# Summing spectral products with accumulating DMAs in a convolution and FFN kernel

## The chip, the cores and the metric

The kernel runs on one core of a Trainium2 chip. The metric is the device time in microseconds (us), as the median of several executions. Every set of runs also executed the kernel before on the same chip; its medians there lay between 374.68 and 375.06 us. A run is fast or slow; only fast runs are compared here. The span of a profile is about 1.9 us shorter than the device time of the same execution.

## The reference, cut to what matters

Two layers, each with a long convolution (A) and a gated feed-forward network (B); 2048 rows of 512 columns, 1792 hidden columns.

```python
k_shift = sum over t of k_pad[:, t:t + S, :] * shift_k[:, ks - 1 - t]     # 4 taps
kv = k_shift * v
y = irfft(rfft(kv, padded) * rfft(ssm_k, padded))[:, :S] + kv * ssm_D
A(q) = q * y
B(x) = (silu(x @ w_gate) * (x @ w_up)) @ w_down
x = q
x = x + A(layernorm(x)); x = x + B(layernorm(x))      # layer 0
x = x + A(layernorm(x)); x = x + B(layernorm(x))      # layer 1
```

y depends on k, v and ssm_k only, so the spectral work is done once and both layers use its result.

## The kernel before

The rows are cut into four chunks of 512. Chunk by chunk the kernel transforms kv (spectrum X) and h (ssm_k; spectra H, combined to G) by matmuls with a small Fourier matrix, multiplies spectra, adds the products that belong to the same output chunk into Z, and transforms Z back. This is interleaved with 16 FFN units (two layers, four chunks, two halves of 256 rows). The program is written as a list of operations; a list scheduler, run while the kernel is built, settles the order on every engine from estimated durations and landing times of DMAs. Buffers come from rings of fixed size.

The spectral product, on VectorE, in short form; `sl` covers the four slots, so each operation is 128x2048:

```python
for part in (0, 1):                       # real, imaginary
    t1 = X.real * G[part]                 # dve tensor_mul
    t2 = X.imag * G[1 - part]             # dve tensor_mul
    comb = ALU.subtract if part == 0 else ALU.add
    if first:                             # the first product of this Z
        Z[part] = t1 comb t2              # dve tensor_tensor
    else:
        t1 = t1 comb t2                   # dve tensor_tensor
        Z[part] = Z[part] + t1            # dve tensor_add
```

The FFN side of VectorE, and the DMA transposes that feed it:

```python
# prologue of a unit: normalised rows z, turned by DMA for the gate and up matmuls
add("SP", 1.25, lambda: nc.sync.dma_start_transpose(out=zT..., in_=z...), lat=1.4, slack=SLK)
...
# unit: 8 matmuls (128x256) per gate or up tile, silu and copy on ScalarE, then
dve(n * W, lambda: nc.vector.tensor_mul(out=ht.t[:], in0=ht.t[:], in1=sg.t[:]), [sg], [ht])
# down projection reads ht
```

h is turned with TensorE and the shift of k is four diagonal matmuls per tile, in all chunks.

Of the kernel before, what the change touches and what calls it, by code (L numbers as in the profile page):

```python
# [19 lines left out]
SLK = 5.0  # L20
PD_ACT, KV_ACT, ST_ACT = True, True, False
HSL = 3.0
Z_ACT, N_ACT = False, False
# [3 lines left out]

BLOCKS = [("C", 0, 1), ("C", 1, 1), ("C", 2, 1), ("C", 3, 1),
# [6 lines left out]
class Buf:  # L35


    def __init__(self, ring, name, make, parts=1):
        self.ring, self.name, self.make, self.parts = ring, name, make, parts
        self.last_write = [None] * parts  # L40
        self.readers = [[] for _ in range(parts)]
        self.ops, self.left, self.free_at, self.t = [], 0, 0.0, None


class Op:
    __slots__ = ("eng", "cost", "lat", "emit", "bufs", "preds", "succs", "due", "fixed", "conv", "left", "end", "start", "n")


class Plan:
# [6 lines left out]
    def __init__(self, rings):  # L56
        self.ops = []
        self.rings = rings
        self.slots = {r: [None] * n for r, n in rings.items()}
        self.queue = {r: [] for r in rings}  # L60
# [6 lines left out]
    def add(self, eng, cost, emit, r=(), w=(), lat=None, due=None, conv=False, slack=0.0):  # L67
        o = Op()
        o.eng, o.cost, o.emit, o.conv, o.n = eng, cost, emit, conv, len(self.ops)
        o.lat, o.fixed, o.due = lat, due, -slack  # L70
        o.preds, o.succs, o.bufs = {}, [], []
# [16 lines left out]
        for b in o.bufs:  # L88
            b.ops.append(o)
            b.left += 1  # L90
        for q in o.preds:
            q.succs.append(o)
        o.left = len(o.preds)
# [8 lines left out]
    def dues(self, stretch, floor):  # L102
        nxt = {}
        for o in reversed(self.ops):
# [4 lines left out]
            if o.conv:  # L109
                d = min(d, nxt.get(o.eng, 1e9) - o.cost * stretch[o.eng])  # L110
                nxt[o.eng] = d
                d = max(d, floor)
            o.due = d - slack

    def order(self, warm_until, warm):
        t = {e: 0.0 for e in self.SAME}
        ready = {e: [] for e in self.SAME}
        for o in self.ops:
            if not o.left:
                ready[o.eng].append(o)  # L120
        done = 0
        heads = {r: 0 for r in self.rings}
        while done < len(self.ops):
            best = None
            for e, cand in ready.items():
                pick = None
                for o in cand:
# [3 lines left out]
                    ok = True  # L131
                    taken = {}
                    for b in o.bufs:
                        if b.t is None and b.ring != "one":
                            qd = self.queue[b.ring]
                            if heads[b.ring] >= len(qd) or qd[heads[b.ring] + taken.get(b.ring, 0)] is not b:
                                ok = False
                                break
                            free = sorted(s.free_at if s is not None else 0.0 for s in self.slots[b.ring]
                                          if s is None or not s.left)  # L140
                            n = taken.get(b.ring, 0)
                            if n >= len(free):
                                ok = False
                                break
                            taken[b.ring] = n + 1
                            est = max(est, free[n] + 0.1 if free[n] else 0.0)
# [10 lines left out]
            e = o.eng  # L157
            if e == "PE" and est < warm_until and est - t[e] > 0.5:
                self.dummy(warm, t[e], est)
            for b in o.bufs:  # L160
                if b.t is None and b.ring == "one":
                    b.t = b.make(0)
                if b.t is None:
                    slot = min((i for i, s in enumerate(self.slots[b.ring]) if s is None or not s.left),
                               key=lambda i: self.slots[b.ring][i].free_at if self.slots[b.ring][i] is not None else 0.0)
                    self.slots[b.ring][slot] = b
                    heads[b.ring] += 1
                    b.t = b.make(slot)
            o.emit()
            o.start, o.end = est, est + o.cost  # L170
            t[e] = o.end
            for b in o.bufs:
                b.left -= 1
                b.free_at = max(b.free_at, o.end + (0.15 if o.lat is None else o.lat))
            ready[e].remove(o)
            for s in o.succs:
                s.left -= 1
                if not s.left:
                    ready[s.eng].append(s)
            done += 1  # L180

    def dummy(self, warm, a, b):
        for ring in ("pf", "pd", "pc"):
            for i, s in enumerate(self.slots[ring]):
                if s is None or (not s.left and s.free_at <= a):
                    n = int((b - a - 0.4) / 0.085)
                    if n > 0:
                        warm(ring, i, n)
                    return
# [3 lines left out]
def kernel(  # L193
# [29 lines left out]
    o_t = out.rearrange("b s d -> (b s) d").rearrange("(c p r) d -> p c r d", p=P, r=R)  # L223
    k3 = A_k.rearrange("b s d -> (b s) d").rearrange("s (dt p) -> s dt p", p=P)
# [7 lines left out]
                 "sg": 2, "ht": 5, "st": 8, "mv": 6, "ve": 6, "rs": 6, "pf": 4, "pc": 2, "pd": 2})  # L232
# [26 lines left out]
    NI = NT // 2  # L259
    m4, fq = whole("m4", [P, R], F32), whole("fq", [P, P], F32)  # L260
# [3 lines left out]
    fwd, inv = whole("fwd", [P, NT, P]), whole("inv", [P, NT, P], parts=2)  # L264
# [8 lines left out]
    hn, kT, vt, xs = {}, {}, {}, {}  # L273

    def load_h(b, eng="SP", due=None):
        hn[b] = new("h", "hn", [P, KD, L], parts=1)
        q = nc.sync if eng == "SP" else nc.scalar
        add(eng, 0.55, lambda: q.dma_start(out=hn[b].t[:], in_=h3[:, :, b * L:(b + 1) * L]), w=[hn[b]], lat=4.5, due=due)

    def load_k(b, due=None):  # L280
        kT[b] = new("k", "kTb", [P, KD, PADL + L], parts=2)
        if b == 0:
            add("POOL", 0.2, lambda: nc.gpsimd.memset(kT[b].t[:, :, 0:PADL], 0.0), w=[(kT[b], (0,))])
            add("SP", 1.5, lambda: nc.sync.dma_start_transpose(out=kT[b].t[:, :, PADL:PADL + L], in_=k3[0:L]),
                w=[(kT[b], (1,))], lat=3.5, due=due)
        else:
            add("SP", 2.2, lambda: nc.sync.dma_start_transpose(out=kT[b].t[:], in_=k3[b * L - PADL:(b + 1) * L]),
                w=[kT[b]], lat=4.0)

    def load_v(b, due=None):  # L290
        vt[b] = new("v", "vt", [P, R, D], parts=R)
        add("SP", 0.6, lambda: nc.sync.dma_start(out=vt[b].t[:], in_=v_t[:, b]), w=[vt[b]], lat=4.5, due=due)

    def load_x(c, due=None):
        xs[c] = new("x", "xc", [P, R, D], parts=R)
        add("SP", 0.7, lambda: nc.sync.dma_start(out=xs[c].t[:], in_=q_t[:, c]), w=[xs[c]], lat=4.5, due=due)
# [91 lines left out]
    def shift_mul(b, ring, conv):  # L388
        for r in range(R):
# [7 lines left out]
            add("PE", pe(KS * KD, P), go, r=[kT[b], dg], w=[ps], conv=conv)  # L397
# [19 lines left out]
    def fold2(src, dst, conv):  # L417

        for lo, op in ((0, ALU.add), (2, ALU.subtract)):
            dve(4 * D, lambda lo=lo, op=op: nc.vector.tensor_tensor(out=dst.t[:, lo:lo + 2], in0=src.t[:, 0:2],  # L420
                                                                    in1=src.t[:, 2:4], op=op),
                [src], [(dst, key((lo, lo + 1)))], conv=conv)
# [14 lines left out]
    def forward4(rows, name, scale, ring, conv):  # L437
        ev = spectrum(name)
        by_residue(rows, ev, scale, ring, ("ACT",), conv)
        m = spectrum("m")  # L440
        fold2(ev, m, conv)
# [4 lines left out]
    def spectrum_h(b, ring="pc"):  # L446
        hs = transpose_h(b, ring, (0, 2), True)
        h, hp = forward4(hs, "H", 2.0 / N, ring, True), H[b - 1]
        H[b] = h
# [5 lines left out]

# [399 lines left out]
```

## Time and profile before

| | before |
|---|---|
| device time, median | 374.69 us |
| span of the profile | 372.8 us |
| first 128x512 gating product (end of unit 1) | 59.73 us |
| from there to the eleventh (units 2 to 11) | 213.8 us |
| units 12 to 16 | 92.6 us |
| tail | 6.6 us |

Each unit ends on VectorE with the one narrow gating product, ht 128x512, so the starts of these sixteen operations cut any of these kernels into comparable pieces. All stage lengths below are read in this way. In the lines of the profile PE is TensorE, PEld its weight loads, DVE VectorE, ACT ScalarE, POOL GpSimd and SP SyncE; a q after the name marks instructions that only issue. zT is z turned by DMA, hs and kc are h and k turned; a transfer's landing is its end, counted here from its issue. In the middle piece spectral work and FFN share the engines; in units 12 to 16 only the FFN is left. The lines of the page and of the views are shown in the prediction below. The page's DMA rows: 40 equal slices of the span; the digit is the busy tenths of the 16 DMA engines, below it what they moved.

```profile
DMA  8995050010210441010100230001100210011100
GB/s 243 402 304 155 9 113 25 2 28 2 51 64 1 87 119 51 3 28 3 28 29 1 43 99 2 2 1 31 29 30 0 58 29 2 14 16 15 43 2 28
```

In slices two and three, 90% busy or more with loads, the DMA engines move 402 and 304 GB/s. After the opening the DMA engines are mostly idle.

### The profile page before, as it was taken

The numbers are of one execution on the slowest core, as the hardware profiler recorded it, in microseconds if no ns is written. First come the engines' busy times: TensorE is split into PE (matmuls) and PEld (weight loads), VectorE is DVE, ScalarE is ACT, GpSimd is POOL, SyncE is SP. The second block draws the span as 40 slices with busy tenths as digits, with TensorE's granted clock in tenths as the row PEclk, the third lists the DMA queues.
The fourth block names the chain that finished last, engine by engine and source line by source line (L and its number), as shares of the span: only waits on it lengthen the run. The fifth ranks groups of instructions, "written<-read, shape, count | busy, mean of one in ns | idle before, by whom it ended". The sixth has DMA issues, their size and how long they took to land.

```text
span 372.8 us, 6865 instructions
## 1 busy us (share of the span) xinstructions
PE 354.1 (95%) x2814; PEld 258.9 (69%) x2814; DVE 292.8 (79%) x542; ACT 209.0 (56%) x363; POOL 36.2 (10%) x42
## 2 busy tenths in 40 slices
PE   7989999979999899998999999997999999999995
PEld 7735877747678567766676687775777777777772
DVE  7895999999989999999999799799974453636121
ACT  3668784536684663635456856744456454545452
POOL 1101010110101300111110100021100100100000
PEclk9999999999999999999999999999999999999999
DMA  8995050010210441010100230001100210011100
GB/s 243 402 304 155 9 113 25 2 28 2 51 64 1 87 119 51 3 28 3 28 29 1 43 99 2 2 1 31 29 30 0 58 29 2 14 16 15 43 2 28
DMA packets 34351, 20.42 MB, mean 55 GB/s; under 512 B 26384, under 2 KB 32272, under 8 KB 34320
## 3 DMA queue, kind: packets, MB, share of 16 engines
q1 hardware_dynamic: 32736, 19.45, 19.9%
q10 hardware_dynamic: 1584, 0.53, 0.6%
q8 instruction: 22, 0.36, 0.4%
q14 instruction: 9, 0.07, 0.1%
HBM read 11.80 MB, written 2.10 MB: 37 GB/s over the span
## 4 chain that ended last, share of the span: by engine, by line
DVE 45%; PE 41%; DMA 4%; POOL 3%; ACT 3%; issue 1%; SPq 1%; ACTq 0%; POOLq 0%
PE pf L255 24%; PE pd L685 12%; DVE bnst L550 6%; DVE m L420 5%; DVE ht L678 5%; PE ps L255 4%; POOL rstd L555 3%; DVE t L486 3%; DVE t L489 3%; DMA hn<-in_A_ssm_k_dram 3%; DVE t L498 2%; DVE Z L500 2%; DVE Z L495 2%; DVE n L598 2%; DVE z L598 2%; DVE xc L695 1%
## 5 line engine op out<-in xcount | busy, mean ns | idle before, releaser
L255 PE MATMUL pf<-zT,wg_sb 128*128 128x256 bf16 x896 | 116.1, 273 | 1.4 <-DMA zT<-z 1.4
L255 PE MATMUL pf<-zT,wu_sb 128*128 128x256 bf16 x896 | 116.1, 273 | 0.0
L685 PE MATMUL pd<-wd_sb,ht 128*128 128x512 bf16 x448 | 106.6, 379 | 8.1 <-DVE ht L678 8.1
L671 ACT ACTIVATE sg<-pf 128x512 bf16<-128x512 f32 x112 | 67.2, 600 | 74.0 <-PE pf L255 69.9
L255 PEld LDWEIGHTS <-wg_sb 128*128 128x128 bf16 x896 | 87.3, 98 | 22.4 <-DMA zT<-z 1.9
L255 PEld LDWEIGHTS <-wu_sb 128*128 128x128 bf16 x896 | 87.6, 98 | 11.8
L675 ACT CAST ht<-pf 128x512 bf16<-128x512 f32 x112 | 65.8, 587 | 27.5 <-PE pf L255 27.5
L685 PEld LDWEIGHTS <-ht 128*128 128x128 bf16 x448 | 42.8, 98 | 54.0 <-DVE ht L678 12.6
L678 DVE TENSOR_TENSOR ht<-ht,sg 128x1024 bf16<-128x1024 bf16 x64 | 39.5, 617 | 37.9 <-ACT ht L675 37.9
L555 POOL TENSOR_TENSOR rstd<-ve,nhalf 128x2 f32<-128x2 f32 (+1 forms) x33 | 35.1, 1064 | 304.6 <-DVE ve L553 304.6
L550 DVE BATCH_NORM_STATS2 bnst<-xc 128x6 f32<-128x512 bf16 x64 | 41.6, 684 | 1.1 <-DMA xc<-in_A_q_dram 0.5
L692 ACT CAST dn<-pd 128x512 bf16<-128x512 f32 x32 | 17.6, 591 | 23.0 <-PE pd L685 23.0
L489 DVE TENSOR_TENSOR t<-X,G 128x2048 bf16<-128x2048 bf16 x18 | 21.9, 1217 | 0.0
L486 DVE TENSOR_TENSOR t<-X,G 128x2048 bf16<-128x2048 bf16 x18 | 21.9, 1216 | 0.0
L325 ACT ACTIVATE X<-ps 128x512 bf16<-128x512 f32 x32 | 18.5, 599 | 5.5 <-PE ps L255 5.4
L695 DVE TENSOR_TENSOR xc<-xc,dn 128x1024 bf16<-128x1024 bf16 x16 | 11.0, 687 | 10.6 <-ACT dn L692 10.5
L598 DVE TENSOR_SCALAR z<-xc,mv,rstd 128x512 bf16<-128x512 bf16 x32 | 11.8, 409 | 7.3 <-POOL rstd L555 7.2
L598 DVE TENSOR_SCALAR n<-xc,mv,rstd 128x512 bf16<-128x512 bf16 x32 | 12.2, 409 | 6.6 <-POOL rstd L555 6.6
L255 PE MATMUL ps<-dg,kTb 128*128 128x128 bf16 x256 | 15.8, 219 | 0.6 <-ACT Yk L542 0.6
L255 PEld LDWEIGHTS <-kTb 128*128 128x128 bf16 x256 | 15.3, 114 | 1.2 <-issue 0.7
L255 PEld LDWEIGHTS <-fwd 128*128 128x128 bf16 x96 | 9.3, 98 | 8.8 <-issue 0.4
L255 PE MATMUL ps<-vt,fwd 128*128 128x512 bf16 x56 | 15.2, 379 | 0.1
(65 smaller groups left out, 260.1 us busy)
## 6 DMA issues: line engine op xcount, KB each, us to landing
vt<-in_A_v_dram SPq DMA_DIRECT2D x4, 512.0 KB, 4.2
xc<-in_A_q_dram SPq DMA_DIRECT2D x4, 512.0 KB, 4.4
out_dram<-xc SPq DMA_DIRECT2D x16, 128.0 KB, 1.8
wg_sb<-in_B_w_gate_dram SPq DMA_DIRECT2D x1, 1792.0 KB, 10.9
wu_sb<-in_B_w_up_dram SPq DMA_DIRECT2D x1, 1792.0 KB, 15.0
wd_sb<-in_B_w_down_dram SPq DMA_DIRECT2D x1, 1792.0 KB, 19.7
hn<-in_A_ssm_k_dram SPq DMA_DIRECT2D x3, 512.0 KB, 3.3
hn<-in_A_ssm_k_dram ACTq DMA_DIRECT2D x1, 512.0 KB, 3.5
```

Of the source, the lines that this page charges most:

```text
L255: nc.tensor.matmul(o, lhsT=lhsT, rhs=rhs, start=(n == 0), stop=(n == len(terms) - 1))
L325: add("ACT", act(D), lambda: nc.scalar.activation(out=view(), in_=ps.t[:], func=ACT.Copy, scale=scale), r=[ps], w=[(buf, keys)], conv=conv)
L420: dve(4 * D, lambda lo=lo, op=op: nc.vector.tensor_tensor(out=dst.t[:, lo:lo + 2], in0=src.t[:, 0:2], in1=src.t[:, 2:4], op=op), [src], [( ...
L486: dve(n * D, lambda t1=t1, part=part: nc.vector.tensor_mul(out=t1.t[:], in0=x.t[:, sl, 0, :], in1=g.t[:, sl, part, :]), [(x, key(slots, (0 ...
L489: dve(n * D, lambda t2=t2, part=part: nc.vector.tensor_mul(out=t2.t[:], in0=x.t[:, sl, 1, :], in1=g.t[:, sl, 1 - part, :]), [(x, key(slots ...
L550: add("DVE", 0.6, lambda st=st, i=i: nc.vector.bn_stats(out=st.t[:], in_=xs[c].t[:, i, :]), r=[(xs[c], (i,))], w=[st])
L555: add("POOL", 0.75, lambda: nc.gpsimd.tensor_tensor(out=rstd.t[:], in0=ve.t[:], in1=nhalf.t[:].to_broadcast((P, n)), op=ALU.pow), r=[ve, n ...
L598: add("DVE", 0.325, lambda: nc.vector.tensor_scalar(out=view(), in0=xs[c].t[:, i, :], scalar1=mv.t[:, o, 0:1], scalar2=rstd.t[:, o:o + 1], ...
L671: add("ACT", act(D), lambda ps=ps, o=o, sg=sg: nc.scalar.activation(out=sg.t[:, o:o + 2, :], in_=ps.t[:], func=ACT.Silu), r=[ps], w=[(sg, ...
L675: add("ACT", act(D), lambda ps=ps, o=o, ht=ht: nc.scalar.copy(out=ht.t[:, o:o + 2, :], in_=ps.t[:]), r=[ps], w=[(ht, (o // 2,))], due=t0 + ...
L678: dve(n * W, lambda sg=sg, ht=ht: nc.vector.tensor_mul(out=ht.t[:], in0=ht.t[:], in1=sg.t[:]), [sg], [ht], due=t0 + k * step - HSL)
L685: nc.tensor.matmul(pds[o].t[:], lhsT=ht.t[:, q, o * P:(o + 1) * P], rhs=wt["d"].t[:, ft, :], start=(ft == 0), stop=(ft == NF - 1))
```

## The change

Its intent is to relieve VectorE. (1) The sums into Z leave VectorE and are made by DMAs that accumulate in their destination, 512 KB each, on GpSimd's queue. (2) h of chunks 1 to 3 is copied by ScalarE into another layout and turned by DMA transposes. (3) The taps of chunk 3's k are scaled on ScalarE, summed on VectorE and turned by DMA. (4) The opening loads chunk 0's k naturally and turns it on TensorE, issues the taps first, moves h of chunk 0 to second place on ScalarE's queue, loads h and k of chunk 1 early, and adds D's column on GpSimd. (5) The scheduler is rewritten (deadlines by chunk, order and issue apart). Core of the diff, most of it left out:

```diff
+H_DMA = lambda b: b in (1, 2, 3)
+K_ACT = lambda b: b in (3,)
+Z_DMA = lambda i, j: True
...
+    def accumulate(z, sl, slots, part, t):
+        add("POOL", 1.3, lambda: nc.gpsimd.dma_start(out=z.t[:, sl, part, :], in_=t.t[:], accum_op=ALU.add),
+            r=[t, (z, key(slots, (part,)))], w=[(z, key(slots, (part,)))], lat=5.0, conv=True)
...  # in product(), batched case
+            if part and first and Z_DMA(i, j):
+                dve(n * D, lambda: nc.vector.tensor_mul(out=z.t[:, sl, 1, :], in0=x.t[:, sl, 0, :], in1=g.t[:, sl, 1, :]), ...)
+                if part and Z_DMA(i, j):
+                    accumulate(z, sl, slots, part, t1)
...
+            if part and Z_DMA(i, j):
+                accumulate(z, sl, slots, part, t2)
...
+                if Z_DMA(i, j):
+                    accumulate(z, sl, slots, part, t1)
+                    continue
...  # opening
-    load_h(0, "ACT", -60)
+    add("ACT", 1.5, lambda: nc.scalar.activation(out=warm1.t[:], in_=nhalf.t[:], func=ACT.Silu), ...)
     add("ACT", 0.5, lambda: nc.scalar.dma_start(out=tapT.t[:], ...), w=[tapT],
-        lat=2.4, due=-59)
+        lat=2.4, due=-60)
+    load_h(0, "ACT", -59)
     load_k(0, -60)
     load_v(0, -59)
     add("ACT", 0.5, lambda: nc.scalar.dma_start(out=dcol.t[:], ...), w=[dcol], lat=3.0, due=-58)
     load_x(0, -58)
     load_weights("g", -57)
+    load_h(1, "SP", -56.5)
+    load_k(1, -56.4)
```

## The prediction

> **What bounds the kernel now.** I read the busy shares first, then the chain that ended last, then the kernel in two stretches, because a share over the whole span mixes stages.
>
> ```profile
> PE 354.1 (95%) x2814; PEld 258.9 (69%) x2814; DVE 292.8 (79%) x542; ACT 209.0 (56%) x363; POOL 36.2 (10%) x42
> DVE 45%; PE 41%; DMA 4%; POOL 3%; ACT 3%; issue 1%; SPq 1%; ACTq 0%; POOLq 0%
> ```
>
> TensorE looks full, yet the chain spends more of the span on VectorE. Matmul busy time hides small gaps, so I count TensorE work by spacing. In the timeline near the end, where TensorE never waits, eight gate matmuls start 0.87 us after the eight before (0.109 us each), and eight down-projection matmuls take 1.73 us (0.216 us each); a 128-column matmul takes 0.0555 us (16 in 0.89 us in the chain). 1792 gate/up and 448 down matmuls are then 292 us, and everything in program order 348 us of the 372.8 us span.
>
> ```profile
> core 0: us, PE busy (x) PEld busy (x) DVE busy (x) ACT busy (x) POOL busy (x), PEclk, DMA share, GB/s
> 59.70:273.60 213.90, 204.79 (x1614) 150.06 (x1611) 201.76 (x342) 120.64 (x212) 25.46 (x20) 1.00 0.13 31
> 273.60:366.20 92.60, 92.22 (x705) 68.90 (x705) 39.37 (x91) 48.79 (x84) 5.55 (x8) 1.00 0.11 21
> ```
>
> The cuts are ends of FFN units. There are 16 (two layers, four chunks, two halves), and each ends on VectorE with the one narrow gating product, ht 128x512: the first starts at 59.73 us, the eleventh at 273.56, the last at 366.20. Ten units take 213.9 us with VectorE busy 94%; the last five take 92.6 us with VectorE 43% and TensorE full. So VectorE sets the pace up to 273 us and TensorE after it. How VectorE does that, at the end of the first unit:
>
> ```profile
> 56.65 1.42 DVE L433 TENSOR_TENSOR X<-m 128x512 bf16<-128x512 bf16 x4
> 58.00 0.68 DVE L678 TENSOR_TENSOR ht<-ht,sg 128x1024 bf16<-128x1024 bf16 x1
> 58.60 1.21 DVE L495 TENSOR_TENSOR Z<-t,t 128x2048 bf16<-128x2048 bf16 x1
> 59.73 0.42 DVE L678 TENSOR_TENSOR ht<-ht,sg 128x512 bf16<-128x512 bf16 x1
> ```
>
> Spectral work and the gating products share one in-order queue without a gap; TensorE's down projection needs ht, so each 1.2 us operation in front of it is paid.
>
> **What the Trainium skill says.** "Perfetto Trace Analysis", Identifying the Most-Contended Engine, calls matmul busy share a poor measure; the trace agrees (the gate group's mean of 273 ns against 109 ns spacing). "DMA: Bandwidth & Descriptors", SWDGE vs HWDGE vs iDMA, says that accumulating during a DMA is possible only on GpSimd's software path; no run here shows it yet. The same page, Anatomy of one DMA, fits a transfer as about 2.0 us plus bytes over 436e3 per us: 3.2 us for 512 KB. As an accumulating one must also read its destination, I estimate 4 to 6 us from issue to landing; loads of that size in this trace take 3.3 to 4.4 us. "SBUF — State Buffer", Who interferes with whom, says that GpSimd's SBUF reads contend with a two-input VectorE operation. The trace agrees: the small pow on GpSimd takes 0.70 us alone and 1.54 us in the busy stretch.
>
> **The change part by part.**
>
> ```profile
> L489 DVE TENSOR_TENSOR t<-X,G 128x2048 bf16<-128x2048 bf16 x18 | 21.9, 1217 | 0.0
> L500 DVE TENSOR_TENSOR Z<-Z,t 128x2048 bf16<-128x2048 bf16 x12 | 14.6, 1220 | 0.2
> L498 DVE TENSOR_TENSOR t<-t,t 128x2048 bf16<-128x2048 bf16 x12 | 14.6, 1217 | 0.2
> L495 DVE TENSOR_TENSOR Z<-t,t 128x2048 bf16<-128x2048 bf16 x6 | 7.3, 1220 | 0.1
> L255 PE MATMUL ps<-dg,kTb 128*128 128x128 bf16 x256 | 15.8, 219 | 0.6 <-ACT Yk L542 0.6
> L377 PE MATMUL pt<-ident,hn 128*128 128x128 bf16 x64 | 4.9, 220 | 1.7 <-DMA hn<-in_A_ssm_k_dram 1.2 <-DVE hn L740 0.4
> ```
>
> Accumulation: nine batched products. Each of the three that start a Z drops one combination; each of the six others drops the real part's add to Z and both imaginary-part adds. That is 3 + 6 x 3 = 21 operations of 1.22 us, 25.6 us off VectorE, and 21 accumulating DMAs of 512 KB onto GpSimd.
>
> Last shifted k: 64 of the 256 shift matmuls go (3.6 us of TensorE); ScalarE gets 16 scalings of about 0.6 us and loses 4 evacuations; VectorE gets three 1.22 us sums (3.7 us); SyncE gets four transposes.
>
> h by DMA: 48 of 64 transposes leave TensorE (2.7 us), 16 for the natural k arrive (0.9 us); ScalarE's six 1.02 us copies become twelve of about 0.6 us; SyncE gets twelve transposes. A transpose pair of zT takes 2.51 us to issue, so 1.25 us each, and 2.4 us to land.
>
> Where this falls depends on the order, so I cut the built program of both kernels at the 16 unit ends and summed per engine: TensorE by the spacings above; ScalarE by its groups' means; VectorE by the groups' means less 0.03 us. (A plain sum of the means is 314 us against 293 us busy, since neighbours overlap by about 0.055 us; I take half of that, the rest standing for small waits.) The larger of the engines is each unit's length.
>
> Units 2 to 11, before: VectorE 20.8, 22.4, 24.0, 21.1, 19.0, 19.5, 20.3, 23.2, 17.7, 20.2; TensorE 18.2, 21.5, 23.7, 20.0, 17.4, 19.1, 21.1, 24.0, 18.5, 18.2. The larger ones sum to 210.6 us; measured 213.8.
> After: VectorE 17.3, 17.7, 22.7, 20.0, 13.7, 17.7, 21.6, 20.5, 19.0, 16.0; TensorE 16.5, 20.0, 23.5, 20.0, 18.2, 19.1, 21.7, 18.2, 19.1, 19.1. Sum 198.5 us. ScalarE's largest is 19.5, in a unit of 23.5. Gain 12.1 us: VectorE falls under TensorE nearly everywhere, and what is left is TensorE's own 195.4 us.
> Units 12 to 16: TensorE 92.8 before (92.6 measured), 91.9 after; gain 0.9 us. The 6.6 us tail stays.
>
> Opening:
>
> ```profile
> 1.73 6.73 PE L821 MATMUL wm<-ident 128*128 128x128 bf16 x80 [1.73 <-POOL ident masks.py:199]
> 6.69 2.50 DVE L736 TENSOR_TENSOR dg<-ident,tapT 128x512 bf16<-128x512 bf16 x4 [1.47 <-DMA tapT<-in_A_shift_k_dram]
> 18.62 0.50 SPq L278 DMA_DIRECT2D hn<-in_A_ssm_k_dram  x1
> 19.22 8.65 SPq L287 DMA_TRANSPOSE kTb<-in_A_k_dram  x1
> ```
>
> Before, shift matmuls start at 11.2 us, after 80 warming matmuls and the taps' late landing. Afterwards k loads naturally, taps are issued first, and 65 warming matmuls remain; VectorE's order (taps' diagonals split around the phases) lets the shift start at perhaps 9 to 10.5. Two things eat this. Four hr copies of 0.6 us sit between X's evacuations on ScalarE (about 1 us). And hs of chunk 1 now comes from four transposes queued on SyncE behind another k transpose, while the DMA engines are above 90% busy to about 30 us. In order, ScalarE's zT copies stand behind seven of H's evacuations, and TensorE's z transposes behind H's matmuls. Such a transpose held the queue 8.65 us, to 27.9 us; I estimate hs's last block at 28.5 + 3 x 1.25 + 2.4 = 34.7 us, FFN start near 37.5 (38.5 before). I put the first unit's end at 58.5 instead of 59.7, gain 1.2 us.
>
> Accumulation waits, my charge: Z for chunk 2 has two serial imaginary-part accumulations, and VectorE's order leaves about 8 us from the first one's operand to the inverse's first fold; at 5 us each that is 2 us of stall. Chunk 3 leaves 4 us for the last one, in a unit with VectorE slack. Total 1.5 us.
>
> Sum: 374.7 - 12.1 - 0.9 - 1.2 + 1.5 = 362.0 us.
>
> **Rivals.** (1) Accumulation latency becomes the bound. For: they are serial per part of Z, and GpSimd's in-order queue puts later pow operations, which every normalisation needs, behind an issue that waits for an earlier landing. Against: most have 8 to 12 us before the next use. At 8 us each instead of 5, five or six such waits of 2 to 3 us give back 12 us: 373 us. (2) SyncE's queue: hs and kc transposes, 5 us per group, stand before zT transposes, which TensorE waits for. Against: in the trace before, that wait is one of 1.4 us in all. Three late ones of 2 us give 368 us. (3) The opening gains its full 2.5 us or more and no accumulation stalls: 359 us. (4) TensorE was the bound all along, only its removed 5.4 us counting: 369 us. Against: VectorE's 94% and
>
> ```profile
> PE pd L685 <- DVE ht L678: 8.1, 10, 1.2
> ```
>
> waits that busy time shows in part only.
>
> **Range and chances.** The unit sums reproduce the kernel before to 3 us in 306, so the middle is sound to about 3 us if nothing new waits; the opening may miss by 2, the accumulations by up to 8 on the slow side. Hence 355 to 369. The 2% line is 367.2: rival 2 or a mild form of rival 1 is needed to miss it. Faster 0.84, within 0.15, slower 0.01.
>
> **What would show it.** Right: 21 accumulating DMAs and no VectorE add to Z in the batched products, VectorE near 271 us busy, units 2 to 11 in 197 to 203 us, landing of Z's DMAs 4 to 6 us, VectorE under 90% there. Wrong: folds of Z waiting for DMA, pow operations on GpSimd waiting for DMA, zT waits of several us, ScalarE waiting for hs at 30 to 37 us, or the first ht 128x512 not before 59 us.

## The result, and the profile after

The changed kernel takes 392.0 us (median of four, 390.39 to 393.52), the kernel before 374.72 us in the same rounds. The ratio is 1.045 (95% interval 1.039 to 1.051). Ratios here are the mean time of one kernel's fast runs over the mean of the other's fast runs of the same rounds, so not quite the ratio of the medians. The change makes the kernel 17 us slower where I had predicted 13 us faster.

The same two lines of the page as before: busy time by engine, and the chain of work that ended last by engine.

```profile
PE 355.3 (91%) x2668; PEld 257.6 (66%) x2703; DVE 274.8 (70%) x520; ACT 217.2 (55%) x384; POOL 58.3 (15%) x63
PE 56%; DVE 17%; DMA 16%; ACT 6%; issue 3%; POOL 1%; SPq 0%; ACTq 0%; POOLq 0%; DVEq 0%
```

VectorE was relieved as planned: 18 us less busy, and its part of the chain fell from 45% to 17%. But DMA, 4% of the chain before, now has 16%. The two stretches, cut as before (us, then busy time of PE, PEld, DVE, ACT, POOL, then granted clock, DMA share, GB/s):

```profile
66.65:292.50 225.85, 203.15 (x1480) 146.13 (x1500) 182.29 (x323) 127.54 (x227) 47.92 (x42) 0.96 0.54 85
292.50:384.90 92.40, 91.77 (x695) 68.82 (x704) 41.09 (x90) 48.71 (x84) 4.84 (x7) 1.00 0.09 21
```

The middle is 12 us longer, not shorter, with VectorE only 81% busy, the DMA engines at 0.54 instead of 0.13, and a granted clock of 0.96 instead of 1.00. The late stretch is unchanged. The opening is 7 us longer (66.65 against 59.73 us). Set against the prediction, which gave 58.5, 203.2 (213.8 - 12.1 + 1.5), 91.7 and 6.6 us:

| stage | before | predicted | after | after less predicted |
|---|---|---|---|---|
| to the end of unit 1 | 59.7 | 58.5 | 66.7 | +8.2 |
| units 2 to 11 | 213.8 | 203.2 | 225.9 | +22.7 |
| units 12 to 16 | 92.6 | 91.7 | 92.4 | +0.7 |
| tail | 6.6 | 6.6 | 6.9 | +0.3 |

Two errors, then. In the middle the list of waits (who waited for what: us in total, times, longest) has lines that did not exist before:

```profile
POOL Z L593 <- DMA Z<-t: 16.6, 3, 8.1
PE pf L326 <- DMA zT<-z: 11.9, 4, 6.3
DVE t L626 <- DMA Z<-t: 6.8, 3, 3.9
DVE vt L581 <- DMA kc<-ka: 6.7, 1, 6.7
POOL rstd L702 <- DMA Z<-t: 4.7, 1, 4.7
```

Some engines wait for the accumulations themselves (Z<-t); VectorE, which writes t, waits for a product's buffer that an accumulation still reads. TensorE waits for transposes of z that have nothing to do with Z. The chain, read at the start of unit 3 (start, us, what; TensorE's gate and up matmuls in the second line), and the DMA rows of just that unit, 84.3 to 111.2 us, in 40 slices of 0.67 us:

```profile
84.14 7.88 DMA zT<-z
92.16 9.26 PE pf L326 x64
...
DMA  8999999999940002999930000000000100000009
GB/s 137 152 195 187 181 125 125 176 195 196 195 70 0 0 0 40 172 178 171 177 43 0 0 0 0 0 0 0 0 0 0 24 0 0 0 0 12 0 0 188
```

A transpose that takes 2.5 us in the median is issued at 84.14 and lands 7.88 us later. For nearly all of these 7.9 us the DMA engines are full, yet they move only 125 to 196 GB/s, about half of what they moved with loads. Then 64 matmuls take 9.26 us; at the 0.109 us spacing of the prediction they would take 7.0 us. Here "TensorE: Matmul & The Clock Gate" of the Trainium skill, Part 1, The HAM clock gate, tells what I had not looked up: after an idle window of about 3.4 us TensorE's clock is halved until it has been busy for about as long. The trace agrees here: after TensorE's wait of 6.3 us the granted clock is 0.50 from 89.7 to 96.5 us (0.87 over the unit). The gap cost TensorE its own length and some 2 us more. Other gaps in these runs fit the page less well; they come with e17.

Medians of DMA landing (KB, us from issue to landing) from the page; the last two lines concern the opening:

```profile
Z<-t POOLq DMA_DIRECT2D x21, 512.0 KB, 6.4
zT<-z SPq DMA_TRANSPOSE x30, 2.5
kc<-ka SPq DMA_TRANSPOSE x4, 6.8
hn<-in_A_ssm_k_dram ACTq DMA_DIRECT2D x1, 512.0 KB, 10.3
dcol<-in_A_ssm_D_dram ACTq DMA_DIRECT2D x1, 1.0 KB, 12.7
```

The accumulations land after 5.4 to 9.0 us. In the opening h of chunk 0 took 10.3 us to land where it took 3.5 before, and D's column, 1 KB, 12.7 us instead of 5.3. In the timeline of the opening GpSimd's addition of it waits, and behind it the transposes of h and the shift matmuls, which start at 17.80 us instead of 11.20:

```profile
14.62 0.21 POOL L907 TENSOR_TENSOR hn<-hn,dcol 128x4 bf16<-128x4 bf16 x1 [12.85 <-DMA dcol<-in_A_ssm_D_dram]
14.89 1.47 PE L466 MATMUL pt<-ident,hn 128*128 128x128 bf16 x12 [2.67 <-POOL hn L907]
```

### The profile page after: what moved, and what is told of

Read it like the earlier page. It is cut to its first block, busy times and chain, and to the rows that moved or that the text cites. A ratio compares the mean times of both kernels' runs of the same rounds, so it can differ in the third digit from the quotient of the medians.

```text
span 391.8 us, 6690 instructions
## 1 busy us (share of the span) xinstructions
PE 355.3 (91%) x2668; PEld 257.6 (66%) x2703; DVE 274.8 (70%) x520; ACT 217.2 (55%) x384; POOL 58.3 (15%) x63
## 3 DMA queue, kind: packets, MB, share of 16 engines
q1 hardware_dynamic: 39504, 21.55, 22.2%
q0 software_dynamic: 11088, 11.01, 20.4%
## 4 chain that ended last, share of the span: by engine, by line
PE 56%; DVE 17%; DMA 16%; ACT 6%; issue 3%; POOL 1%; SPq 0%; ACTq 0%; POOLq 0%; DVEq 0%
PE pf L326 34%; PE pd L836 13%; PE ps L326 7%; DMA zT<-z 5%; DMA Z<-t 4%; DMA dcol<-in_A_ssm_D_dram 3%; DMA kc<-ka 2%; DVE t L626 2%; DVE m L509 2%; DVE bnst L697 2%; DVE t L632 2%; PE ps L685 2%; DMA hs<-hr 1%; ACT ka L569 1%; DVE ht L829 1%
## 5 line engine op out<-in xcount | busy, mean ns | idle before, releaser
L326 PE MATMUL pf<-zT,wg_sb 128*128 128x256 bf16 x896 | 119.2, 277 | 14.6 <-DMA zT<-z 11.9
L326 PE MATMUL pf<-zT,wu_sb 128*128 128x256 bf16 x896 | 118.9, 277 | 0.1
L326 PEld LDWEIGHTS <-wg_sb 128*128 128x128 bf16 x896 | 88.5, 99 | 38.2 <-issue 10.6
L836 PE MATMUL pd<-wd_sb,ht 128*128 128x512 bf16 x418 | 100.2, 379 | 3.1 <-DVE ht L829 1.6
L326 PEld LDWEIGHTS <-wu_sb 128*128 128x128 bf16 x896 | 88.9, 99 | 15.0 <-issue 1.4
L702 POOL TENSOR_TENSOR rstd<-ve,nhalf 128x2 f32<-128x2 f32 x32 | 29.5, 923 | 202.8 <-DVE ve L700 194.3
L593 POOL DMA_DIRECT2D Z<-t x21 | 27.6, 1320 | 85.7 <-DVE t L632 21.6
L632 DVE TENSOR_TENSOR t<-X,G 128x2048 bf16<-128x2048 bf16 x18 | 21.9, 1219 | 2.0 <-DMA Z<-t 1.9
L626 DVE TENSOR_TENSOR t<-X,G 128x2048 bf16<-128x2048 bf16 x15 | 18.3, 1218 | 6.8 <-DMA Z<-t 6.8
L326 PE MATMUL ps<-vt,fwd 128*128 128x512 bf16 x55 | 15.5, 396 | 5.1 <-DVE vt L581 5.0
L414 ACT ACTIVATE H<-ps 128x512 bf16<-128x512 f32 x24 | 13.7, 612 | 4.7 <-PE ps L326 4.7
L745 DVE TENSOR_SCALAR z<-xc,mv,rstd 128x512 bf16<-128x512 bf16 x32 | 12.1, 414 | 3.7 <-POOL rstd L702 3.7
```

The source lines that it names most:

```text
L326: nc.tensor.matmul(o, lhsT=lhsT, rhs=rhs, start=(n == 0), stop=(n == len(terms) - 1))
L414: add("ACT", act(D), lambda: nc.scalar.activation(out=view(), in_=ps.t[:], func=ACT.Copy, scale=scale), r=[ps], w=[(buf, keys)], conv=conv)
L593: add("POOL", 1.3, lambda: nc.gpsimd.dma_start(out=z.t[:, sl, part, :], in_=t.t[:], accum_op=ALU.add), r=[t, (z, key(slots, (part,)))], w= ...
L626: dve(n * D, lambda t1=t1, part=part: nc.vector.tensor_mul(out=t1.t[:], in0=x.t[:, sl, 0, :], in1=g.t[:, sl, part, :]), [(x, key(slots, (0 ...
L632: dve(n * D, lambda t2=t2, part=part: nc.vector.tensor_mul(out=t2.t[:], in0=x.t[:, sl, 1, :], in1=g.t[:, sl, 1 - part, :]), [(x, key(slots ...
L702: add("POOL", PW, lambda: nc.gpsimd.tensor_tensor(out=rstd.t[:], in0=ve.t[:], in1=nhalf.t[:].to_broadcast((P, n)), op=ALU.pow), r=[ve, nha ...
```

## The experiments

Theory A: the accumulations crowd other transfers out. All 16 DMA engines are full of them while they run, and transposes that TensorE or VectorE waits for land several us late. ("DMA: Bandwidth & Descriptors" of the skill, Issuing engines are not separate DMA queues, says that DMAs of all issuing engines run on the same 16 DMA engines and interleave.) Theory D: what costs is the wait for an accumulated Z. Rivals: SyncE's own queue (theory B), the turning by DMA, the new order, the opening.

Lengths of the stages in the profiles that the arguments below use (e15 and e7 are left out, as their profiles fell in the slow state); "sum" is the end of unit 11. The cut between the first two columns shifts a little with the order, as spectral work moves across it, so kernels of different order are best compared by the sum.

| kernel | time, median | unit 1 ends | units 2-11 | sum | 12-16 |
|---|---|---|---|---|---|
| before | 374.69 | 59.7 | 213.8 | 273.5 | 92.6 |
| after | 392.0 | 66.7 | 225.9 | 292.6 | 92.4 |
| e1_no_accum | 383.22 | 72.2 | 209.8 | 282.0 | 93.1 |
| e2_accum_only | 386.40 | 64.3 | 218.7 | 283.0 | 94.9 |
| e3_opening_only | 376.00 | 66.5 | 208.3 | 274.7 | 92.7 |
| e4_opening_mended | 371.03 | 59.8 | 208.3 | 268.1 | 92.7 |
| e5_accum_mended | 379.94 | 57.0 | 219.9 | 276.9 | 94.9 |
| e8_turned_mended | 374.12 | 63.4 | 209.8 | 273.1 | 92.6 |
| e9_small_accum | 365.51 | 57.1 | 207.2 | 264.4 | 92.6 |
| e11_changed_small | 371.56 | 67.0 | 202.6 | 269.6 | 93.3 |
| e13_ring_full | 378.47 | 58.7 | 217.6 | 276.3 | 96.6 |
| e14_ring_small | 365.32 | 57.1 | 207.1 | 264.2 | 92.7 |
| e16_real_part_only | 372.89 | 58.9 | 212.0 | 270.9 | 92.7 |
| e17_unread_full | 377.04 | 62.4 | 214.2 | 276.6 | 92.6 |
| e18_unread_small | 371.69 | 60.7 | 210.3 | 271.0 | 92.7 |

### The parts alone

e1 is the changed kernel without accumulations, e2 without the DMA turning of h and k, e3 with all three off, so only the opening and the scheduler are new.

```diff
 # e1 and e3 (on the changed kernel)
-Z_DMA = lambda i, j: True
+Z_DMA = lambda i, j: False
 # e2 and e3
-H_DMA = lambda b: b in (1, 2, 3)
+H_DMA = lambda b: False
-K_ACT = lambda b: b in (3,)
+K_ACT = lambda b: False
```

> The changed kernel with the 21 accumulating DMAs undone (VectorE adds into Z again); h and the last k still turned by DMA, new opening kept. Theory A (the accumulations fill the 16 DMA engines, and the transposes on whose landing TensorE waits stand behind them): no zT transpose lands later than 3 us after its issue in the middle (7.4 to 7.9 us in the changed kernel), but VectorE gets its 25 us back and sets the pace again: units 2 to 11 take 212 to 218 us, total 380 to 386 us. Theory B (the hs and kc transposes ahead in SyncE's own queue delay zT, with or without accumulations): the late zT stay, units 2 to 11 take 222 us or more, total 388 us or more. Both: the first unit still ends at 65 to 67 us, since the opening is unchanged.

> The changed kernel with the accumulations kept, h and the last k turned on TensorE again (no hs and no kc transposes). Theory A: zT transposes beside an accumulation still land after 6 to 8 us and TensorE still waits for them; only the 8 us wait for kc is gone: units 2 to 11 take 212 to 220 us, total 378 to 386 us. Theory B: with the queue free the zT waits vanish and the gain I had predicted for the middle appears, 200 to 205 us, total 366 to 372 us.

> All three DMA parts undone: only the new opening and the new planner's order remain. If the opening alone costs about 7 us (late landing of h and of the D column): first unit ends at 64 to 67 us, units 2 to 11 as in the kernel before (212 to 216 us), total 378 to 382 us. If the opening's loss came from the DMA-turned hs of chunk 1 instead: first unit ends at 58 to 61 us, total 372 to 376 us.

Measured: e1 383.22 us (ratio 1.021), e2 386.40 (1.029), e3 376.00 (1.003). Each of the two kinds of DMA adds time to e3: accumulations alone 10.4 us, turning alone 7.2 us. e3's middle is 5.5 us shorter than before's although no operation has left VectorE; the rewritten order alone brings this. Its opening is as long as the changed kernel's, so the opening needs neither kind of DMA to be slow. Theory B asked for a middle of 222 us or more in e1 and 200 to 205 in e2; measured are 209.8 and 218.7, so SyncE's queue is not the main cause. Theory A's numbers missed too: e1's middle is shorter than its 212 to 218 us and its first unit ended at 72.2 instead of 65 to 67 us, and I had expected e3's middle as long as before's.

### The opening

```diff
 # e4 (on e3)
-    load_h(0, "ACT", -59)
+    dcol load on ACT, straight after tapT
     load_k(0, -60)
+    load_h(0, "SP", -59.5)          # second on SyncE, after k
     load_v(0, -59)
-    dcol load on ACT
 # e12 (on e3): only the dcol load moves, to before h, both on ACT
```

> As the run with only the opening, but the D column is loaded right after the taps and h goes second on SyncE's queue, behind k. If the opening loses its time to the D column (12.7 us to landing, behind h on ScalarE's queue, and h itself 10.3 us): h's transposes start by 7 to 8 us instead of 11.6 and 14.9, the first unit ends at 57 to 60 us, total 370 to 375 us. If something else sets the opening: little change, within 2 us of the run with only the opening.

> The run with only the opening, and only one thing moved: the D column is issued before h on ScalarE's queue (h stays third there). If the late D column alone (13 us to landing) cost the opening: first unit ends at 59 to 61 us, total 369 to 375 us, as with both moved. If h's own slow landing beside SyncE's loads (10.3 us) sets it: first unit ends at 62 to 66 us, total 373 to 376 us.

Measured: e4 371.03 us (369.30 to 373.89, ratio 0.989, interval 0.983 to 0.995), e12 376.09 (1.002). The chain in e12's opening, then in e4's:

```profile
1.78 13.76 DMA hn<-in_A_ssm_k_dram
```

```profile
11.37 3.95 PE ps L326 x65
```

With D's column first, the 512 KB of h on ScalarE's queue simply end the wait instead, landing 13.76 us after issue beside SyncE's loads; unit 1 of e12 ends at 68.0 us, later than either expectation. With both loads moved (e4), h second on SyncE's own queue, the shift matmuls start at 11.37 us and unit 1 ends at 59.8. Moving h alone was not tried. The mended opening is then no shorter than before's; it has only lost its loss.

### Accumulations on the mended opening

e5 is e4 with accumulations. e6 is e5 with z turned on TensorE instead of DMA, to take SyncE's transposes away. e7 is e5 with plain copies, e9 with the transfers cut to 16 of 512 columns, e10 with the scheduler told 8.0 instead of 5.0 us for the landing. e8 is e4 with h of chunks 2 and 3 and k of chunk 3 turned by DMA.

```diff
 # e5 (on e4)
-Z_DMA = lambda i, j: False
+Z_DMA = lambda i, j: True
 # e6 (on e5)
-    add("SP", 1.25, ... nc.sync.dma_start_transpose(out=zT..., in_=z...), lat=1.4, slack=SLK)
+    add("PE", pe(KD, P), turn, r=[z, ident], w=[pt], slack=SLK)      # nc.tensor.transpose
+    add("ACT", act(D), ... nc.scalar.copy(out=zT..., in_=pt...), slack=SLK)
 # e7 (on e5)
-    nc.gpsimd.dma_start(out=z.t[:, sl, part, :], in_=t.t[:], accum_op=ALU.add)
+    nc.gpsimd.dma_start(out=z.t[:, sl, part, :], in_=t.t[:])
 # e8 (on e4)
-H_DMA = lambda b: False
+H_DMA = lambda b: b in (2, 3)
-K_ACT = lambda b: False
+K_ACT = lambda b: b in (3,)
 # e9 (on e5)
-    nc.gpsimd.dma_start(out=z.t[:, sl, part, :], in_=t.t[:], accum_op=ALU.add)
+    nc.gpsimd.dma_start(out=z.t[:, sl, part, 0:16], in_=t.t[:, :, 0:16], accum_op=ALU.add)
 # e10 (on e5)
-    ... lat=5.0, conv=True)
+    ... lat=8.0, conv=True)
```

e7, e9 and later e11, e14 and e15 sum wrongly; they came back as correct all the same, so the tolerance does not see these sums, and only their times are used.

> The accumulations on top of the mended opening, h and k turned on TensorE: the base for the next two. Theory A (accumulations crowd the transposes): units 2 to 11 take 215 to 221 us as in the run with the accumulations alone (218.7), against 208.3 without them; the first unit ends at 58 to 61 us; total 376 to 382 us. If the accumulations had only hurt through the late opening: units 2 to 11 at 200 to 206 us, total 362 to 367 us.

> The same, but z is turned by TensorE through PSUM and copied by ScalarE, so no DMA transpose is left in the middle; the 21 accumulations stay. Theory A (the cost is the transposes' late landing): TensorE's waits for zT go, at a price of 8 more 128-column matmuls per unit (0.44 us each unit, 4.4 us over units 2 to 11): units 2 to 11 take 202 to 210 us, total 364 to 372 us. Rival D (the cost is the wait for Z's own landing and GpSimd's queue): units 2 to 11 stay at 214 us or more, total 375 us or more.

> As the mended base with accumulations, but the 21 transfers are plain copies on the same GpSimd queue with the same shapes; the result is wrong on purpose. If the accumulating itself (reading the destination too) makes them long: landing falls from 6.2 to 4 to 5 us, the data rate in them rises from 190 to over 300 GB/s, the latest zT lands within 5 us, units 2 to 11 take 205 to 212 us, total 366 to 373 us. If any 512 KB transfer on that path does it: landing stays at 5.5 us or more and units 2 to 11 stay at 214 us or more.

> No accumulations, mended opening, h of chunks 2 and 3 and the last k turned by DMA (h of chunk 1 on TensorE). Theory A: transposes without accumulations beside them land in 2.4 to 4 us and cost nothing: units 2 to 11 take 205 to 210 us, total 366 to 371 us, equal to the mended opening alone (371.0) or better, as TensorE loses 5.4 us of work in units where VectorE mostly sets the pace. Theory B (their queue delays zT): units 2 to 11 at 213 us or more, total 374 us or more.

> The mended base with accumulations, each transfer cut to 16 of 512 columns per slot (wrong result on purpose): the order of every instruction on VectorE, TensorE, ScalarE and SyncE is the same, the 21 issues, their waits and GpSimd's queue stay, only the bytes go. My prediction took transfers as nearly free. Theory A or D (the transfers' time costs, by crowding or by being waited for): units 2 to 11 take 199 to 206 us instead of 219.9, the first unit ends near 57 us, total 360 to 367 us. If something else in the new order costs (GpSimd's issuing, the order itself): total 372 us or more.

> The mended base with accumulations, planned with a landing of 8.0 us for them instead of 5.0 (measured: 5.4 to 9.5). If the loss is that the order left too little time for Z's own landings (theory D): units 2 to 11 fall to 205 to 212 us, total 366 to 373 us. If it is the crowding of other transfers (theory A), which the planner does not know of: units 2 to 11 stay at 214 to 222 us, total 375 us or more, and zT still lands late by 3 to 5 us several times.

e5 took 379.94 us (1.014), 8.9 us more than e4. e6 took 475.50 us (1.267; its result was correct) and is of no use as a test. Its waits:

```profile
PE ptz L778 <- DVE z L745: 51.5, 8, 15.5
```

TensorE's in-order queue stood for up to 15.5 us before each transpose until VectorE had written z. I put this down to where the scheduler placed the transposes, which was not tested; the run says nothing on the theories.

e7 took 373.26 us (median of its three fast runs, 0.996). The page's landing line:

```profile
Z<-t POOLq DMA_DIRECT2D x21, 512.0 KB, 3.6
```

The same bytes from the same queue, copied and not accumulated, land in 3.6 instead of 5.9 us (median of e5) and cost 6.7 us less in all. e9, same order, hardly any bytes, took 365.51 us (0.975, interval 0.973 to 0.977). So in e5 the accumulations' bytes cost 14.4 us, and what the accumulations save VectorE is worth some 4 to 5.5 us (e4 less e9: 3.7 by the sums of the table, 5.5 by the medians; their orders differ). The order and GpSimd's 21 issues are the same in e5 and e9, so they are not what makes e5 slow. e10 took 377.37 us (1.006): a planner that knows the longer landing wins back 2.6 us, and TensorE still waits for zT.

e8 took 374.12 us (0.999), 3.1 us more than e4. Turning by DMA without any accumulation beside it does not pay either. e8's total fits theory B (374 or more), but not its cause: the middle is 209.8 us, as theory A had it, and TensorE waited for zT once, for 1.0 us. By the spans 3.5 of the 4.9 us lie before the end of unit 1 (63.4 against 59.8 us). In units 2 and 3 the weight loads of TensorE waited up to 7.0 us for ht; I did not follow this further, so why turning costs is open.

### The bytes in the changed kernel itself

e11 is the changed kernel, every part of it, with accumulations of 16 columns (the edit of e9). The order on TensorE, VectorE, ScalarE and SyncE is identical.

> The changed kernel itself, opening and turned h and k included, with the accumulations cut to 16 columns (wrong result on purpose). Theory A: zT, hs and kc transposes now land in 2.4 to 4 us, no 8 us wait for kc or zT is left, units 2 to 11 take 201 to 210 us instead of 225.9, the first unit still ends at 65 to 68 us, total 370 to 377 us. Theory B (SyncE's queue of transposes): the waits for kc and zT stay, units 2 to 11 at 216 us or more, total 384 us or more.

It took 371.56 us (0.991, interval 0.989 to 0.993): 20.4 us less than the changed kernel by the medians, 22.2 us by the spans (391.8 and 369.6). Its middle is 202.6 us, 23.3 us less. The chain at the start of unit 3, to be set beside the two lines shown above:

```profile
84.51 2.71 DMA zT<-z
87.22 0.14 issue
87.36 3.67 PE pf L326 x32
```

The same transpose lands in 2.71 instead of 7.88 us, and 32 matmuls take 3.67 us, nearly full speed. Unit by unit, three of the ten units carry 18.6 of the 23.3 us:

| unit | after | e11 | difference | what lands late in the changed kernel |
|---|---|---|---|---|
| 3 | 26.9 | 19.9 | +7.0 | zT, 7.88 us |
| 7 | 24.2 | 19.5 | +4.7 | zT, 7.04 us |
| 10 | 28.8 | 21.9 | +6.9 | kc, 8.04 us (3.50 in e11) |
| other seven | 146.0 | 141.3 | +4.7 | |

All three are transposes on SyncE's queue, not Z. Z<-t stands on the changed kernel's chain too, at 147.72 for 8.98 us and at 203.21 for 6.65 us, but the units in which these waits lie (5 and 8) are no more than 1.1 us longer than e11's. A wait on the chain of one run need not be what a change costs: without it, something else may end nearly as late. The same caution holds for unit 7: there VectorE also waited 3.9 us for a product's buffer and GpSimd 7.7 us for an earlier landing, so its 4.7 us are not zT's alone for certain.

### Crowding or waiting

e13, e14 and e15 share one order of e5's kind, with the ring of zT cut from three buffers to two. e14 cuts the accumulations to 16 columns. e15 does too, and sends the other 480 columns of the same product into a buffer that nobody reads.

```diff
 # e13, e14, e15 (on e5)
-RINGS = {}
+RINGS = {"zT": 2}
 # e15: each accumulation becomes two
+    nc.gpsimd.dma_start(out=z.t[:, sl, part, 0:16], in_=t.t[:, :, 0:16], accum_op=ALU.add)
+    nc.gpsimd.dma_start(out=junk.t[:], in_=t.t[:, :, 0:480], accum_op=ALU.add)
```

> e5 with a ring of two buffers for zT, so that the transposes of one z can be issued while the previous zT is still read. It is the yardstick of the next two runs. Theory A (the accumulations' bytes crowd the other transfers out): the zT transposes still land up to 6 to 8 us after their issue, total 376 to 383. Theory D (what costs is the wait for an accumulated Z itself): the same, 376 to 383, with waits on Z of 10 us and more. A third possibility (zT's buffer was freed too late): 368 to 374, and no zT wait over 3 us.

> e13 in the same order with the accumulations cut to 16 of 512 columns (wrong sums on purpose). Theories A and D both: 363 to 370, zT at most 4.5 us from issue to landing. If it stayed above 374, the order and not the bytes would be what costs in e13.

> e13 in the same order on TensorE and SyncE; each accumulation into Z is cut to 16 columns and a second one carries the other 480 columns of the same product into a buffer that nobody reads, so the bytes are all there and nothing waits for them (wrong sums on purpose; the products' buffers are still held until they are read). Theory A: nearly all of the cost stays, 373 to 383, with zT landing 5 to 8 us after issue. Theory D: nearly all of it goes, 364 to 370, with zT still late now and then but nothing lost by it. Between, 370 to 373: both.

The expectation of e13 has an error: the ring was made smaller, to make room for e15's buffer, not larger as the text says. The third possibility that it names was therefore not tested. e13 took 378.47 us (1.010), e14 365.32 (0.975), which repeats e5 and e9. The chains of the two at the same places, first e13, then e14:

```profile
164.84 5.84 DMA zT<-z
170.82 8.81 PE pf L326 x64
...
253.69 5.53 DMA zT<-z
...
274.35 5.44 DMA zT<-z
```

```profile
160.62 2.62 DMA zT<-z
163.38 7.15 PE pf L326 x64
...
244.54 2.53 DMA zT<-z
```

The three late transposes open units 7, 11 and 12 of e13, which are 4.9, 3.0 and 3.9 us longer than e14's: 11.8 us of the spans' difference of 16.0 (13.2 by the medians). Three waits for Z<-t on e13's chain (5.58, 8.38 and 5.84 us, between 79.9 and 104.9 us) lie around units 3 and 4, which are 3.0 us longer together. Another 1.6 us is not due to the accumulations at all: the 80 shift matmuls of the opening took 8.81 instead of 7.19 us in that execution.

e15 took 390.17 and 394.22 us in its two fast runs (1.045), more than e13, so neither theory's number. The waits, from a slow run, show why:

```profile
POOL junk L593 <- DMA junk<-t: 25.1, 8, 4.0
DVE t L632 <- DMA junk<-t: 8.0, 5, 2.9
```

The second transfers waited for each other on GpSimd and held the products' buffers, which VectorE then waited for. The test made waits of its own and is inconclusive.

e17 and e18 avoid this. They are e4, with all sums on VectorE, smaller rings to make room, and 21 accumulations of a resident weight into two spare buffers in turn, 432 columns in e17 and 16 in e18. Nobody reads them and they hold no product; a one-column copy on GpSimd makes each wait until the product at its place is there.

```diff
 # e17 and e18 (on e4), called where an accumulation into Z would stand
+    def unread(t):
+        def go():
+            nc.gpsimd.tensor_copy(out=pace.t[:], in_=t.t[:, 0, 0:1])
+            nc.gpsimd.dma_start(out=spare[...][:, :, 0:432], in_=wt["d"].t[:, 0:4, 0:432], accum_op=ALU.add)   # e18: 0:16
+        add("POOL", 1.5, go, r=[t], conv=True)
```

> The control of the next run. The mended opening without any accumulation into Z (the sums stay on VectorE), with smaller rings to make room (two buffers for z and zT, four for ht), and 21 small accumulations (16 columns) of a resident weight into spare buffers that nobody reads, each issued by GpSimd when the product at whose place it stands is there. 370 to 375, zT at most 4.5 us from issue to landing; above 376 the smaller rings would cost by themselves.

> The same kernel in the same order with these 21 accumulations at 432 of 512 columns, 432 KB each: nobody reads them and they hold no product. Theory A (crowding): slower than the control by most of 84% of the 13 us between e13 and e14, 7 to 12 us, with transposes of z that land 5 to 8 us after their issue and waits of TensorE for them. Theory D (waiting for Z itself): within 2 us of the control. Between 2 and 7: both, about halved.

e18 took 371.69 us (0.992), e17 377.04 (1.004, interval 1.001 to 1.008). (e18's latest zT landed after 5.4 us, not within the 4.5 expected.) The difference, 5.3 us, lies between the two theories' numbers. The profiles show where it is. Units 4 to 16 are equal to within 0.2 us in both; unit 1 ends 1.7 us later in e17, because 65 shift matmuls before any accumulation took 5.57 instead of 3.95 us; and unit 3 is 26.9 us in e17, 22.8 in e18. Unit 3 in both (e17 first), and what starts it in e17 (PE's timeline):

```profile
83.50:110.40 26.90, 23.05 (x161) 16.48 (x164) 21.66 (x37) 13.61 (x24) 4.78 (x5) 0.87 0.30 47
```

```profile
81.80:104.60 22.80, 22.24 (x161) 16.03 (x164) 21.65 (x37) 13.64 (x24) 4.78 (x5) 0.93 0.14 19
```

```profile
88.28 1.87 PE L326 MATMUL pf<-zT,wg_sb 128*128 128x256 bf16 x8 [3.25 <-DMA zT<-z]
89.94 1.91 PE L326 MATMUL pf<-zT,wu_sb 128*128 128x256 bf16 x8
91.64 1.83 PE L326 MATMUL pf<-zT,wg_sb 128*128 128x256 bf16 x8
93.31 1.04 PE L326 MATMUL pf<-zT,wu_sb 128*128 128x256 bf16 x8
94.18 1.04 PE L326 MATMUL pf<-zT,wg_sb 128*128 128x256 bf16 x8
```

A transfer that nobody reads made TensorE wait 3.25 us for zT, and the next groups of eight matmuls started 1.66 to 1.70 us apart instead of 0.87. The control has the same order and no such wait, so this is crowding, and it cost 4.1 us. It happened once in 21 transfers; probably only one transpose that TensorE needed at once stood beside an accumulation in this order, which I did not check. Elsewhere the same transfers cost nothing that shows.

The half clock does not follow from the length of one gap. In the control two groups started 1.55 and 1.71 us apart at the same place, after waits of only 1.46 and 1.89 us for ht. In e13 TensorE waited 3.89 us for zT, up to 259.26 us, and the groups after it kept 0.87 us. So a gap is sometimes paid twice here and sometimes once.

### Keeping a part

e16 is e4 with six accumulations only, the real parts of the products that are added to a Z.

```diff
 # e16 (on e4)
-                if Z_DMA(i, j):
+                if Z_DMA(i, j) or part == 0:
                     accumulate(z, sl, slots, part, t1)
                     continue
```

> The mended opening with six accumulations only (the real parts of the products that are added to a Z), instead of none (371.0) or 21 (379.9). If the cost goes with the number of accumulations: 371 + 6/21 x 9 = about 373.5. If a few of them can be put where nothing waits: 367 to 371, which would make it the fastest of all. Neither theory is decided by it; it asks whether some of the change can be kept.

It took 372.89 us (0.994, interval 0.991 to 0.997), 1.9 us more than e4 and near the 373.5 that the count alone gives, but the two intervals overlap (e4 0.983 to 0.995), so the difference is not clear of noise. Its chain in unit 9 has

```profile
199.98 5.96 DMA zT<-z
```

Six accumulations are enough for one to meet a transpose of z. No version with whole accumulations had a lower median than e4, which has the lowest of the kernels that sum rightly (e18's interval overlaps with it): 1% faster than before, under the 2% that would count as faster, on its own order and with none of the three DMA parts.

## Why the prediction was wrong, point by point

**VectorE's relief: right.** I expected VectorE near 271 us busy, under 90% in the middle; it was 274.8 and 81%. The removed operations and the 21 accumulations are there.

**Middle by unit sums: right for the engines, wrong for the kernel.** The step "The larger of the engines is each unit's length" gave 198.5 us, 201.7 with the 3.2 us by which the same sum missed before. e11, with the same order and no bytes, measured 202.6. What failed is the assumption that nothing but the four engines can set a unit's length. Also, the 12.1 us gain was not all relief: the new order alone, with nothing relieved, gave 5.5 us (e3, e4).

**"Accumulation waits, my charge ... Total 1.5 us": wrong, and the main error.** The same term measured 23.3 us (e11 against after). I had charged only the readers of Z for the landing of Z. The landing itself, 5.4 to 9.0 us with a median of 6.4, was above my 4 to 6, but not by much. The larger part was not a wait for Z on the chain: 18.6 us fell in three units that began with a late transpose of z or k (with the caution on unit 7), and e17 shows that a transfer nobody reads can do this. Theory A is shown as a mechanism. How the whole splits between A and D is not settled for the changed kernel: 4.7 us lie in the other seven units. In e13 some 12 us stand against 3. The half clock added to some of the late transposes: in unit 3 64 matmuls took 9.26 us, not 7.0.

**Rivals.** Rival 1 named GpSimd's waits for earlier landings, and they came (16.6 us). One of 8.1 us lies in unit 5, which is only 1.1 us longer than e11's; the other long one, 7.7 us, lies in unit 7 and cannot be told apart from the late zT there. The one late pow (4.7 us) lies in unit 11, 1.0 us longer. Rival 2 had the symptom, late zT waits, but the wrong cause: SyncE's queue order. In e11 the queue has the same order and zT lands in at most 3.8 us. I argued against it with the trace before, where the wait was 1.4 us in all; but that trace had DMA engines 13% busy, and the change itself filled them. The evidence was from a state that the change removed.

**Opening: wrong by 8.2 us.** "VectorE's order ... lets the shift start at perhaps 9 to 10.5" took the loads' landing times from before. I did notice that the engines are full in the opening, and used it only for chunk 1's h. h of chunk 0, moved behind the taps on ScalarE's queue while SyncE issued five loads, landed in 10.3 instead of 3.5 us; mending the two loads gave the loss back (e4). e12 shows that moving D's column alone is not enough.

**Units 12 to 16 and the tail: right,** within 1 us.

**Range and chances.** The 8 us allowed for accumulations was a bound on waits for Z; the error came by a way that the range did not hold. Slower, which came, had a chance of 0.01.

## What to carry to other kernels

Before moving work to DMA, ask what else uses the DMA engines in that stretch and who waits for it: a transfer's cost is not only its own landing but the delay of small urgent transfers beside it, and TensorE may pay a gap twice, once idle and once at half clock (after 3.25 us in e17, though not after 3.89 us in e13). To price such a transfer, run the changed kernel with its transfers cut to a few columns in the same order; the difference is the price of its bytes, and no share of the critical chain gives it. And measure a rewritten scheduler with the other parts switched off before crediting its gain to them.

## What the Trainium skill lacked or had wrong

- "DMA: Bandwidth & Descriptors": no rate for accumulating transfers. Here 512 KB within SBUF landed in 5.9 us (median in e5, 6.4 in the changed kernel, up to 9.0), against 3.6 us for a plain copy of the same bytes; the fit of its section Anatomy of one DMA gives 3.2. The engines were full at 125 to 196 GB/s.
- The same page, Issuing engines are not separate DMA queues: right that all interleave, but without a figure for what a small transfer pays. Here a transpose of 2.5 us took 5.4 to 8.0 us beside an accumulation; without any, the latest zT took 3.8 (e1) to 4.6 us (e3).
- The same page has no figure for how a load on ScalarE's queue fares beside several on SyncE's: 512 KB went from 3.5 to 10.3 us and 13.8 us (e12), 1 KB to 12.7 us.
- "TensorE: Matmul & The Clock Gate", Part 1: its idle window of about 3.4 us does not tell here when the clock is halved. After a gap of 3.25 us (e17), and in e18 after gaps of only 1.46 and 1.89 us, groups of eight matmuls started 1.55 to 1.71 us apart; after gaps of 1.16 us (e11) and 3.89 us (e13) they kept the usual 0.87.
